# Retention and a gated feed-forward on one core: another order of the ramp, with the powers for q taken from the mask's first row

## Chip, core and metric

The kernel runs on one core of a Trainium2 chip. Its engines are TensorE (PE: matrix products; PEld is its weight load), VectorE (DVE), ScalarE (ACT), GpSimd (POOL) and SyncE (SP, which here only issues DMAs). The metric is the device time of one execution in microseconds (us), as the median of several runs.

## What is computed

Retention in blocks with a decay per head, then RMS norm and a gated feed-forward over its output:

```python
Dmask = np.where(rel >= 0, lam[:, None, None] ** rel[None], 0.0)
lam_pow = lam[:, None, None] ** (pos[None, :, None] + 1)
for b in range(nb):
    intra = np.einsum('bhic,bhjc->bhij', qb, kb) * Dmask[None]
    intra = np.einsum('bhij,bhjd->bhid', intra, vb)
    inter = np.einsum('bhid,bhde->bhie', qb * lam_pow[None], kv_state)
    out[:, :, sl] = intra + inter
    kv_state = lam_block[None, :, None, None] * kv_state + np.einsum(
        'bhsd,bhse->bhde', kb * rev_pow[None], vb)
xn = x / np.sqrt(np.mean(x * x, axis=-1, keepdims=True) + 1e-06) * rms_g
g, val = xn @ w_gate, xn @ w_val
y = (g / (1.0 + np.exp(-g)) * val) @ w_out
```

4 sequences of 768 tokens, 8 heads of 64, a model width of 512 and an inner width of 1536, all float32.

## The kernel before

The 3072 tokens are cut into six groups m of 512, each of four chunks of 128; the heads into four pairs p; the inner width into twelve blocks f of 128. A `Pair(m, p)` does the retention of one group and pair of heads: `scores` (PE, tile pa), `decay_a` (DVE multiplies pa by the mask), `decay_k` (ACT), `decay_q` (POOL, in some places DVE, multiplies q by the powers pw), `state_sums` (PE, pst), `states` (DVE: a copy and multiply-adds), `mix_chunks` and `mix_states` (PE, both into po), `keep_output` and `keep_squares` (po to x and to its squares). `Norm(m)` sums the squares over the heads, takes the root (POOL, a power) and has PE spread it over the partitions (pr); `scaled`, `high` and `low` make the two fp16 parts of x. `Weights(f)` converts the float32 weights of a block, which arrive as pairs of words, into two fp16 parts: `lift` (ACT), `convert` (DVE), `square` (ACT), `norm` (PE, pn), `scale` (DVE), `high` (ACT), `low` (DVE), `undo` (DVE, the factors cg that the silu takes). `Hidden(m, f)` multiplies: `gate` and `val` are twelve fp16 products each, in three parts of four (high by high, low by high, high by low), `silu` and `mul` join them, and `out(t)` multiplies by the block of w_out, one output tile t at a time.

Weights and the first two groups are prepared in a ramp, the function `ramp()`, in which every call stands by itself. It runs under a manual schedule: each engine has one queue and runs its instructions in the order in which `ramp()` issues them, and an instruction that waits holds all behind it on its engine. After the ramp the loop over `unit()` runs the other products; `load_next()` issues the next load on SP's queue.

The places that matter here (lines of the kernel before):

- L155 `powers(p, part)`: parts 0 and 1 are the mask of the pair's two heads, part 2 the powers pw of the pair for q; all twelve are scans on DVE. pw's scans read a tile of zeros that ACT makes (L215).
- L142 `busy(n)`: n products of the identity with itself, which nothing reads.
- L179 to L197 `largest`, `scales`, `scales_of`: the largest norm gain gives the scales gs and cx; `scales_of` is seven small DVE operations.
- L597 `Norm.sums`: for group 0 the squares of pairs 0, 1 and 2 are added first (POOL and DVE, L583), and the two that are left are summed over partitions by products 128 columns wide (`n = 1 if self.m else P`).
- L787 `h1.mul(True)` and L711: h1 isn't split into a high and a low part; its `out` is one float32 product per tile, the others take three products (L714 to L716).

```python
            queue = nc.scalar if m == 0 and p == 0 and i else nc.sync
        n = 1 if self.m else P
```

Of the kernel before, what the change touches and what calls it, by code (L numbers as in the profile page):

```python
# [17 lines left out]
P = 128  # L18
# [5 lines left out]
def retention_swiglu_kernel(  # L24
# [117 lines left out]
    def busy(n):  # L142

        ps = ps_out.tile([P, DM], F32, tag="po2", name="unread")
        for _ in range(n):
            nc.tensor.matmul(ps[:, :P], ident, ident, start=True, stop=True)  # L146
# [8 lines left out]
    def powers(p, part):  # L155
        if part < 2:
            h = 2 * p + part
            nc.vector.tensor_tensor_scan(
                mask[:, h, :], lam_b[:, h : h + 1].broadcast_to([P, P]), ident, 0.0,
                ALU.mult, ALU.add,  # L160
            )
        else:
            nc.vector.tensor_tensor_scan(
                pw[:, p, :], lam_p[:, p : p + 1].broadcast_to([P, P]), zeros, 1.0,
                ALU.mult, ALU.add,
            )
# [23 lines left out]
    def scales_of(pmax):  # L190
        nc.vector.tensor_reduce(gmax, pmax[:, :P], axis=mybir.AxisListType.X, op=ALU.max)
        nc.vector.tensor_single_scalar(ge, gmax.bitcast(I32), 0x7F800000, op=ALU.bitwise_and)
        nc.vector.tensor_scalar_min(ge, ge, float(252 * EXP))
        nc.vector.tensor_scalar(sx.bitcast(I32), ge, -1.0, float(253 * EXP), ALU.mult, ALU.add)
        nc.vector.tensor_scalar(gs, gcol, sx, XS, ALU.mult, ALU.mult)
        nc.vector.tensor_scalar_add(cx.bitcast(I32), ge, float(EXP))
        nc.vector.tensor_scalar_mul(cx, cx, 1.0 / (XS * WS))  # L197
# [15 lines left out]

    zeros = wg[:, NF - 1, 1].bitcast(F32)[:, :P]
    nc.scalar.mul(zeros, ones, 0.0)  # L215
# [141 lines left out]
    class Weights:  # L357
# [79 lines left out]
        def undo(self):  # L437
            inv = small.tile([P, 2], F32, tag="inv", name=f"inv_{self.f}")
            nc.vector.tensor_scalar_add(inv.bitcast(I32), self.e2, float(64 * EXP))
            nc.vector.tensor_scalar_mul(cg[:, self.f, :], inv, cx)  # L440
# [19 lines left out]
    class Pair:  # L460
# [48 lines left out]
        def states(self):  # L509
            m, p = self.m, self.p  # L510
            for c in range(GC):
# [4 lines left out]
                if g % SEQ_CH == 0:  # L516
                    nc.vector.tensor_copy(new, self.pst[:, c, :])
                else:
# [49 lines left out]
        def keep_squares(self):  # L568
# [4 lines left out]
            if m and p == 0:  # L573
# [10 lines left out]

    class Norm:


        def __init__(self, m):
            self.m = m
            self.x, self.sq = rows.pop(m)  # L590
# [6 lines left out]
        def sums(self, i=0):  # L597

            if i == 0:
                if self.m:  # L600
                    pss = ps_att.tile([P, 2, G], F32, tag="ps", name=f"pss_{self.m}")[:, 0]
                else:
                    pss = ps_out.tile([P, DM], F32, tag="po2", name=f"pss_{self.m}")
                self.pss = pss
            sq = self.sq[i]

            n = 1 if self.m else P
            for c in range(GC):
                nc.tensor.matmul(  # L609
                    self.pss[:, c * n : (c + 1) * n], sq[:, c, :], ones[:, :n],  # L610
                    start=i == 0 and c == 0, stop=bool(i or self.m), skip_group_check=True,
                )
            self.pss4 = self.pss[:, : GC * n].rearrange("p (c i) -> p c i", c=GC)[:, :, 0]

        def mean(self):
            m = self.m
            self.ms = small.tile([P, GC], F32, tag="ms", name=f"ms_{m}")
            nc.vector.tensor_scalar(self.ms, self.pss4, 1.0 / DM, 1e-6, ALU.mult, ALU.add)
# [197 lines left out]
    def ramp():  # L816
# [4 lines left out]
        p00, p01, p02, p03, p10, p11, p12, p13 = (Pair(m, p) for m in range(2) for p in range(NP))  # L821
        largest()
        pm = scales()
        powers(0, 0)
        powers(2, 0)
        powers(0, 1)
        powers(1, 1)
        powers(2, 1)
        powers(3, 2)
        powers(3, 1)  # L830
        p00.decay_k()
        busy(5)
        powers(1, 0)
        powers(3, 0)
        powers(0, 2)
        powers(1, 2)
        powers(2, 2)
        p00.scores()
        busy(4)
        p00.decay_a()  # L840
        p00.decay_q(nc.gpsimd)
        p01.decay_k()
        p00.state_sums()
        p00.states()
        p01.scores()
        p01.decay_a()
        scales_of(pm)
        p01.state_sums()
        p01.states()
        p00.mix_chunks()  # L850
        p00.mix_states()
        p02.scores()
        p02.decay_a()
        p02.decay_k()
        p02.state_sums()
        p02.states()
        p01.mix_chunks()
        p01.decay_q(nc.gpsimd)
        p01.mix_states()
        p03.scores()  # L860
        p03.decay_a()
        p00.keep_output(nc.scalar)
        p02.decay_q(nc.gpsimd)
        p00.keep_squares()
        p03.decay_k()
        p03.state_sums()
        p03.states()
        p03.decay_q(nc.gpsimd)
        p01.keep_output(nc.scalar)
        p01.keep_squares()  # L870
        p02.mix_chunks()
        p02.mix_states()
        w0.lift()
        p03.mix_chunks()
        p03.mix_states()
        p02.keep_squares()
        p01.add_squares(nc.gpsimd)
        p02.add_squares(nc.vector)
        w0.convert(part=0)
        w0.convert(part=1)  # L880
        load_next()
        p03.keep_squares()
        p03.keep_output(nc.scalar)
        p02.keep_output(nc.scalar)
        load_next()
        n0 = Norm(0)
        n0.sums(0)
        n0.sums(1)
        w0.square(0)
        n0.mean()  # L890
        w1.lift(0)
        w1.lift(1)
        p10.scores()
        load_next()
        p10.decay_a()
        busy(3)
        busy(8)
        w1.convert(0)
        w0.square(1)
        w0.pn = w1.pn = ps_out.tile([P, DM], F32, tag="po3", name="pn_0")  # L900
        w0.norm()
        w1.convert(1)
        w1.square(0)
        p10.decay_k()
        w0.scale()
        n0.root()
        n0.spread()
        w1.square(1)
        w1.pn = w0.pn[:, 2:]
        w1.norm(slice(0, 1))  # L910
        n0.scaled(0)
        n0.high(0)
        p10.state_sums()
        n0.scaled(1)
        p10.states()
        n0.scaled(2)
        w0.high(0)
        n0.high(1)
        n0.scaled(3)
        w0.low(0)  # L920
        n0.high(2)
        n0.high(3)
        n0.low(1, nc.vector)
        w1.scale(slice(0, 1))
        p10.mix_chunks()
        w0.high(1)
        w0.low(1)
        w0.lift_o()
        w1.high(0)
        n0.low(3, nc.vector)  # L930
        n0.low(2, nc.vector)
        w0.undo()
        w1.low(0)
        w1.pn = ps_att.tile([P, 2, G], F32, tag="ps", name="pn_1")[:, 0]
        w1.norm(slice(1, 2))
        p10.decay_q(nc.gpsimd)
        p10.mix_states()
        h0.gate(0)
        h0.gate(1)
        h0.val(0)  # L940
        w2.lift()
        h0.val(1)
        w1.lift_o()
        n0.low(0, nc.gpsimd)
        h0.gate(2)
        w2.convert(part=0)
        h0.val(2)
        w1.scale(slice(1, 2))
        h0.silu()
        w2.convert(part=1)  # L950
        w1.high(1)
        h0.mul()
        w1.low(1)
# [373 lines left out]
```

## Time and profile before

| | |
|---|---|
| time, median of 3 runs | 678.54 us (677.96 to 679.63) |
| profiled execution, its own time | 678.86 us |
| its span, first to last instruction | 677.1 us |
| mean granted clock of TensorE over the span | 0.999 of full speed |
| busy: PE, DVE, ACT, POOL | 668.6, 328.9, 248.6, 64.1 us |

A busy time is the sum of the times in which an engine has an instruction in work. PE's records overlap (the ends of products are modelled), so the step from one start to the next says what a product costs. A row of the timeline has the start, the time from start to end, engine, line and operation, the tiles (out<-in), sizes and count; in brackets is how long the engine was idle before, and what ended that. Every float32 product is two records in such a row.

### The profile page before, as it was taken

What the parts mean: (1) busy time and instruction counts of PE and PEld (TensorE: products, weight loads), DVE (VectorE), ACT (ScalarE), POOL (GpSimd) and SP (SyncE); (2) the same over time, 40 slices, a digit from 0 to 9 for tenths busy, and PEclk for the clock granted to TensorE, in tenths of its full rate; (3) what the DMA queues carried; (4) which work ended last, traced back from release to release, by engine and by line L of the source; (5) the groups of instructions that cost most, each with busy time, mean ns of one, the idle gap of its engine ahead of it and who ended that gap; (6) DMA issues with size and microseconds to landing.
All of it is one profiled execution on the core that took longest, in us unless ns stands there. A gap on an engine that the chain in (4) does not pass through costs nothing.

```text
span 677.1 us, 9894 instructions
## 1 busy us (share of the span) xinstructions
PE 668.6 (99%) x4138; PEld 362.6 (54%) x4138; DVE 328.9 (49%) x591; ACT 248.6 (37%) x439; POOL 64.1 (9%) x59
## 2 busy tenths in 40 slices
PE   7999999999999999999999999999999999999997
PEld 6845665555566655554444555444465444444443
DVE  6797866466567486453812312641332462211112
ACT  3687635455446324454213222231332231211111
POOL 2300000000012002343000111000012000000000
PEclk9999999999999999999999999999999999999999
DMA  8937802234015101122001132100100000100001
GB/s 312 370 122 277 271 19 99 101 110 153 38 63 178 71 0 63 64 85 104 1 0 46 32 111 67 60 0 1 63 1 1 1 0 1 63 0 1 0 1 62
DMA packets 14301, 50.97 MB, mean 75 GB/s; under 512 B 1713, under 2 KB 1969, under 8 KB 12849
## 3 DMA queue, kind: packets, MB, share of 16 engines
q1 hardware_dynamic: 13968, 49.69, 20.8%
q10 hardware_dynamic: 288, 0.66, 0.3%
q8 instruction: 32, 0.52, 0.3%
q14 instruction: 13, 0.10, 0.0%
HBM read 44.05 MB, written 6.29 MB: 74 GB/s over the span
## 4 chain that ended last, share of the span: by engine, by line
PE 98%; DVE 1%; DMA 0%; ACT 0%; issue 0%; DVEq 0%
PE pg L695 28%; PE pv L695 28%; PE acc L714 10%; PE acc L716 9%; PE acc L715 9%; PE pa L475 4%; PE po L535 3%; PE po L546 3%; PE pst L504 2%; PE unread L146 1%; PE acc L711 1%; DMA cs<-in_consts_dram 0%; PE pss L609 0%; DVE xn L673 0%; PE pr L631 0%; PE pss L645 0%
## 5 line engine op out<-in xcount | busy, mean ns | idle before, releaser
L695 PE MATMUL pg<-x,wg 128*128 128x512 f16 x864 | 199.8, 379 | 0.6 <-ACT x L678 0.6
L695 PE MATMUL pv<-x,wv 128*128 128x512 f16 x864 | 199.5, 379 | 0.0
L787 DVE SCALAR_TENSOR_TENSOR sg<-pv,cv,sg 128x512 f32<-128x512 f32 x48 | 36.0, 750 | 219.6 <-PE pv L695 219.6
L695 PEld LDWEIGHTS <-wv 128*128 128x128 f16 x864 | 84.1, 98 | 100.4 <-issue 1.1
L695 PEld LDWEIGHTS <-wg 128*128 128x128 f16 x864 | 82.3, 98 | 102.9 <-issue 6.1
L716 PE MATMUL acc<-wo,hh 128*128 128x512 f16 (+1 forms) x284 | 109.1, 384 | 0.0
L715 PE MATMUL acc<-wo,hh 128*128 128x512 f16 (+1 forms) x284 | 109.0, 384 | 0.0
L780 ACT ACTIVATE sg<-pg,cg 128x512 f32<-128x512 f32 x72 | 49.4, 685 | 152.3 <-PE pg L695 152.2
L797 ACT CAST hh<-sg 128x512 f16<-128x512 f32 (+1 forms) x71 | 43.9, 618 | 166.1 <-DVE sg L787 166.1
L714 PE MATMUL acc<-wo,hh 128*128 128x512 f16 x192 | 72.9, 380 | 0.0
L495 POOL TENSOR_TENSOR qkv<-qkv,pw 128x512 f32<-128x512 f32 x21 | 27.0, 1285 | 299.3 <-PE pa L475 299.3
L804 DVE TENSOR_TENSOR hh<-sg,hh 128x512 f16<-128x512 f32 x48 | 33.8, 704 | 24.6 <-ACT hh L797 24.6
L714 PE MATMUL acc<-wo,hl 128*128 128x512 f32 x92 | 40.6, 441 | 0.0
L491 DVE TENSOR_TENSOR a<-pa,mask 128x1024 f32<-128x1024 f32 x24 | 29.4, 1224 | 7.6 <-PE pa L475 7.4
L714 PEld LDWEIGHTS <-hh 128*128 128x128 f16 x192 | 18.8, 98 | 23.5 <-issue 2.4
L716 PEld LDWEIGHTS <-hh 128*128 128x128 f16 x192 | 18.8, 98 | 22.7
L787 DVE SCALAR_TENSOR_TENSOR sg<-pv,cg,sg 128x512 f32<-128x512 f32 x23 | 17.2, 748 | 27.3 <-PE pv L695 25.7
L715 PEld LDWEIGHTS <-hh 128*128 128x128 f16 x192 | 18.8, 98 | 20.8
L475 PE MATMUL pa<-qkv 64*128 64x128 f32 x384 | 28.8, 291 | 0.0
L475 PEld LDWEIGHTS pa<-qkv 64*128 64x128 f32 x384 | 24.1, 193 | 8.3 <-issue 7.0
L535 PE MATMUL po<-a,qkv 128*64 128x128 f32 x384 | 25.3, 274 | 0.0
L566 ACT COPY x<-po 128x512 f32<-128x512 f32 x24 | 13.8, 582 | 29.4 <-PE po L546 29.3
(132 smaller groups left out, 615.4 us busy)
## 6 DMA issues: line engine op xcount, KB each, us to landing
qkv<-in_qkv_dram SPq DMA_DIRECT2D x47, 512.0 KB, 5.0
raw_gv<-in_weights_dram SPq DMA_DIRECT2D x11, 1024.0 KB, 6.2
raw_o<-in_weights_dram SPq DMA_DIRECT2D x12, 512.0 KB, 4.0
out_dram<-o SPq DMA_DIRECT2D x23, 256.0 KB, 2.3
partial<-in_weights_dram SPq DMA_DIRECT2D x2, 512.0 KB, 12.5
qkv<-in_qkv_dram ACTq DMA_DIRECT2D x1, 512.0 KB, 4.1
out_dram<-o SPq DMA_DIRECT2D x1, 128.0 KB, 2.1
out_dram<-o ACTq DMA_DIRECT2D x1, 128.0 KB, 2.0
```

The costliest lines, as they stand in the source:

```text
L475: nc.tensor.matmul(self.pa[:, j, c, :], self.kT[r, c, :], self.qT[r, c, :], start=True, stop=True,)
L491: nc.vector.tensor_mul(self.a, self.pa, decay.broadcast_to([P, 2, GC, P]))
L495: eng.tensor_mul(self.qT, self.qT, pw[:, p : p + 1, :].broadcast_to([P, GC, P]))
L535: nc.tensor.matmul(po[r, c, :], self.v[:, c, r], self.a[:, j, c, :], start=c == 0, stop=False, skip_group_check=True,)
L695: nc.tensor.matmul(ps, w[:, kk, :], x[:, kk, :], start=i == kk == 0, stop=i == 2 and kk == NK - 1,)
L714: nc.tensor.matmul(acc, hl[:, ts_], oh, start=first, stop=False)
L715: nc.tensor.matmul(acc, hh[:, ts_], ol, start=False, stop=False)
L716: nc.tensor.matmul(acc, hh[:, ts_], oh, start=False, stop=last)
L780: nc.scalar.activation(self.sg, self.pg, AF.Silu, scale=cg[:, self.f, 0:1])
L787: nc.vector.scalar_tensor_tensor(out, self.pv, factor, self.sg, ALU.mult, ALU.mult)
L797: nc.scalar.copy(self.hh, self.sg)
L804: nc.vector.tensor_sub(self.hl, self.sg, hh)
```

## The change

- **Loads.** Of the first pair's two transfers, qT and kT now go on ACT's queue and k and v on SP's; before it was the other way about.
- **Powers for q.** `spread_powers(p)` has PE multiply the identity's first column, broadcast to 64 columns, by the mask of each of the pair's heads: two products of 64x128, whose result is the mask's first row (powers 0 to 127) on all partitions of a head. `powers_of` lets ACT multiply it by lam into pw. The four DVE scans and the tile of zeros go.
- **Small operations.** `scales_of` (five of seven operations) goes to GpSimd, and so do four of the twelve `undo`s and four `low_o`s (the low part of w_out).
- **Row sums.** `row_sums(m, i)` sums each pair's squares by products one column wide, for group 0 with all four pairs summed on PE: sixteen products in place of eight wide ones, and no `add_squares` for group 0.
- **First weights by halves.** w0 is lifted, converted, squared and scaled half by half (w1 already was).
- **First states.** `first_state` copies a sequence's first state by itself, in five places on ACT.
- **h1** is split like the others (`h1.mul()`, `h1.high()`, `h1.low()`).
- **Fillers** (`busy`): fifteen products in place of twenty, two and five of them ahead of everything else.
- **The order** of all calls in `ramp()` is new.

```diff
-            queue = nc.scalar if m == 0 and p == 0 and i else nc.sync
+            queue = nc.scalar if m == p == i == 0 else nc.sync
...
+    def spread_powers(p):
+        ps = ps_out.tile([P, DM], F32, tag="po3", name=f"pp_{p}")
+        for j, r in enumerate(heads):
+            nc.tensor.matmul(
+                ps[r, :P], ident[:, 0:1].broadcast_to([P, D]), mask[:, 2 * p + j, :], start=True, stop=True
+            )
+        return ps
+
+    def powers_of(p, ps):
+        nc.scalar.mul(pw[:, p, :], ps[:, :P], lam_p[:, p : p + 1])
...
-    zeros = wg[:, NF - 1, 1].bitcast(F32)[:, :P]
-    nc.scalar.mul(zeros, ones, 0.0)
...
+    def row_sums(m, i):
...
+        for c in range(GC):
+            nc.tensor.matmul(
+                pss[m][:, c : c + 1], rows[m][1][i][:, c, :], ones[:, :1],
+                start=i == 0 and c == 0, stop=bool(i == NP - 1 or m), skip_group_check=True,
+            )
...
         largest()
+        powers(3)
+        busy(2, 3)
...
-        h1.mul(True)
...
+        h1.mul()
```

Three places in the order follow: PE at the start, PE from the first group's sums to the first gate, and POOL. Names: unread is a filler, pmax the spread of the largest gain, pa scores, pp the spread powers, pst state sums, po outputs, pss row sums, pn the weights' squared norm, pr the spread root, pg the gate.

PE at its start, before:

```order
L187 MATMUL pmax<-ident,gmax 128x128
L146 MATMUL unread<-ident 128x128 x5
L475 MATMUL pa_0_167<-qkv_0_97 128x128 x8
L146 MATMUL unread<-ident 128x128 x4
L504 MATMUL pst_0_186<-qkv_0_97 64x64 x8
L475 MATMUL pa_1_199<-qkv_1_100 128x128 x8
```

and with the change:

```order
L146 MATMUL unread_146<-ident 128x128 x2
L146 MATMUL unread_150<-ident 128x128 x5
L192 MATMUL pmax<-ident,gmax 128x128
L479 MATMUL pa_0_164<-qkv_0_97 128x128 x8
L146 MATMUL unread_175<-ident 128x128 x2
L165 MATMUL pp_181<-mask,ident 64x128 x2
L508 MATMUL pst_0_185<-qkv_0_97 64x64 x8
```

Seven fillers, which need only the identity, stand ahead of pmax, which needs the constants; the first powers stand behind the first scores.

PE from the last pair's outputs to the first gate (pg), before:

```order
L546 MATMUL po_3_339<-qkv_3_106,state 64x128 x6
L609 MATMUL pss_371<-ones,sq_0_301 128x128 x4
L609 MATMUL pss_371<-ones,sq_3_363 128x128 x4
L475 MATMUL pa_0_389<-qkv_0_360 128x128 x8
L146 MATMUL unread<-ident 128x128 x11
L411 MATMUL pn_421<-ssq_380,ones 128x2
L631 MATMUL pr_436<-ident,y_434 128x128 x4
L411 MATMUL pn_421<-ssq_425,ones 128x1
L504 MATMUL pst_0_447<-qkv_0_360 64x64 x6
L535 MATMUL po_0_473<-a_0_402,qkv_0_360 64x128 x8
L411 MATMUL pn_492<-ssq_425,ones 128x1
L546 MATMUL po_0_473<-qkv_0_360,state 64x128 x6
```

and with the change (the first four products of pg follow):

```order
L558 MATMUL po_3_345<-qkv_3_106,state 64x128 x6
L608 MATMUL pss_297<-ones,sq_1_289 128x1 x4
L608 MATMUL pss_297<-ones,sq_2_379 128x1 x4
L608 MATMUL pss_297<-ones,sq_3_381 128x1 x4
L146 MATMUL unread_402<-ident 128x128 x2
L415 MATMUL pn_405<-ssq_383,ones 128x1 x2
L642 MATMUL pr_426<-ident,y_419 128x128 x4
L479 MATMUL pa_0_433<-qkv_0_280 128x128 x8
L508 MATMUL pst_0_446<-qkv_0_280 64x64 x6
L415 MATMUL pn_405<-ssq_453,ones 128x1
```

The spread root stands ahead of the next group's scores, nine fillers are gone here, and the next group's po comes only after part 0 of the gate.

POOL from the constants on, before:

```order
L495 TENSOR_TENSOR qkv_0_97<-qkv_0_97,pw 128x512
L495 TENSOR_TENSOR qkv_1_100<-qkv_1_100,pw 128x512
L495 TENSOR_TENSOR qkv_2_103<-qkv_2_103,pw 128x512
L495 TENSOR_TENSOR qkv_3_106<-qkv_3_106,pw 128x512
L583 TENSOR_TENSOR sq_0_301<-sq_0_301,sq_1_320 128x512
L622 TENSOR_TENSOR y_434<-ms_383,power 128x4
L495 TENSOR_TENSOR qkv_0_360<-qkv_0_360,pw 128x512
L681 TENSOR_TENSOR x_298<-xn_0_444,x_298 128x512
```

and with the change, from the last two of the five operations of `scales_of` on (which stand between the q of pair 2 and that of pair 3):

```order
L203 TENSOR_SCALAR cx<-ge 128x1
L204 TENSOR_SCALAR cx<-cx 128x1
L499 TENSOR_TENSOR qkv_3_106<-qkv_3_106,pw 128x512
L633 TENSOR_TENSOR y_419<-ms_417,power 128x4
L443 TENSOR_SCALAR inv_458<-e_0_421 128x2
L444 TENSOR_SCALAR cg<-inv_458,cx 128x2
L692 TENSOR_TENSOR x_272<-xn_3_444,x_272 128x512
L692 TENSOR_TENSOR x_272<-xn_2_456,x_272 128x512
L499 TENSOR_TENSOR qkv_0_280<-qkv_0_280,pw 128x512
L443 TENSOR_SCALAR inv_595<-e_1_473 128x2
L444 TENSOR_SCALAR cg<-inv_595,cx 128x2
L257 TENSOR_TENSOR wo_637<-wg,wo_637 128x512
```

Behind the root POOL has two low parts of x in place of one, the factors of w0 and w1, and the low part of the first w_out.

## Rows read from the trace of the kernel before

**Rows 1.** The page's busy times; waits of PE (waited for, total, times, longest).

```profile
PE 668.6 (99%) x4138; PEld 362.6 (54%) x4138; DVE 328.9 (49%) x591; ACT 248.6 (37%) x439; POOL 64.1 (9%) x59
...
PE pmax L187 <- DVE gmax L180: 3.9, 1, 3.9
PE pg L695 <- ACT x L678: 0.6, 2, 0.3
```

**Rows 2.** Timeline, 0 to 10 us: POOL makes the identity, then PE.

```profile
1.12 0.29 POOL masks.py:199 TENSOR_SCALAR_AFFINE_SELECT ident<-ident 128x128 f32<-128x128 f32 x1
...
4.44 2.34 PE L146 MATMUL unread<-ident 128*128 128x128 f32 x10
6.71 2.08 PE L475 MATMUL pa<-qkv 64*128 64x128 f32 x16
8.72 1.54 PE L146 MATMUL unread<-ident 128*128 128x128 f32 x8
```

**Rows 3.** Timeline, PE over one pair, 17.5 to 22 us.

```profile
17.58 1.16 PE L475 MATMUL pa<-qkv 64*128 64x128 f32 x16
...
19.19 1.05 PE L535 MATMUL po<-a,qkv 128*64 128x128 f32 x16
20.16 0.87 PE L546 MATMUL po<-qkv,state 64*64 64x128 f32 x12
20.97 1.09 PE L535 MATMUL po<-a,qkv 128*64 128x128 f32 x16
```

**Rows 4.** Timeline, PE at the first norm, 22 to 30 us.

```profile
22.79 2.05 PE L609 MATMUL pss<-ones,sq 128*128 128x128 f32 x16
...
25.87 3.04 PE L146 MATMUL unread<-ident 128*128 128x128 f32 x22
...
29.06 1.13 PE L631 MATMUL pr<-ident,y 128*128 128x128 f32 x8
```

**Rows 5.** Timeline, the other engines at the first norm, 25 to 32 us.

```profile
25.19 1.03 POOL L622 TENSOR_TENSOR y<-ms,power 128x4 f32<-128x4 f32 x1 [3.83 <-DVE ms L618]
...
30.23 1.40 DVE L673 SCALAR_TENSOR_TENSOR xn<-x,gs,pr 128x512 f32<-128x512 f32 x2 [0.41 <-PE pr L631]
...
31.01 0.62 ACT L678 CAST x<-xn 128x512 f16<-128x512 f32 x1 [0.30 <-DVE xn L673]
...
31.70 1.16 POOL L681 TENSOR_TENSOR x<-xn,x 128x512 f16<-128x512 f32 x1 [4.23 <-ACT x L678]
```

**Rows 6.** Timeline, PE's first products, 32 to 42 us.

```profile
32.73 0.61 PE L695 MATMUL pg<-x,wg 128*128 128x512 f16 x2
...
34.29 1.24 PE L695 MATMUL pg<-x,wg 128*128 128x512 f16 x5 [0.28 <-ACT x L678]
...
38.90 2.75 PE L695 MATMUL pg<-x,wg 128*128 128x512 f16 x12
```

**Rows 7.** Timeline, PE: h1's outputs, narrow row sums of group 1, three-part outputs.

```profile
63.19 1.88 PE L711 MATMUL acc<-wg,h 128*128 128x512 f32 x4
...
81.66 0.95 PE L609 MATMUL pss<-ones,sq 128*128 128x1 f32 x8
82.47 0.48 PE L714 MATMUL acc<-wo,hl 128*128 128x512 f32 x1
...
83.24 0.39 PE L714 MATMUL acc<-wo,hl 128*128 128x512 f32 x1
```

**Rows 8.** Timeline, DVE and POOL, 260.5 to 263 us.

```profile
260.62 0.75 DVE L264 SCALAR_TENSOR_TENSOR rest<-wo,ts,wo 128x512 f32<-128x512 f32 x1
...
261.52 1.27 POOL L267 TENSOR_TENSOR wo<-rest 128x512 f16<-128x512 f32 x1 [28.39 <-DVE rest L264]
...
262.22 1.12 DVE L264 SCALAR_TENSOR_TENSOR rest<-wo,ts,wo 128x512 f32<-128x512 f32 x1 [0.85 <-ACT wo L262]
```

**Rows 9.** DMA issue of w0's two halves on SP's queue.

```profile
5.40 1.24 SPq L98 DMA_DIRECT2D partial<-in_weights_dram  x2
```

**Rows 10.** DMA issues of 5.3 to 5.9 us: KB each, us to landing.

```profile
partial<-in_weights_dram SPq DMA_DIRECT2D x1, 512.0 KB, 12.3
```

More of the change, by code (lines that the diff above doesn't have):

```diff
@@ L889, in ramp @@
-        w0.square(0)
         n0.mean()
-        w1.lift(0)
-        w1.lift(1)
-        p10.scores()
-        load_next()
-        p10.decay_a()
[L896 to L908, printed above, removed]
+        n0.root()
+        w0.scale(slice(0, 1))
@@ new lines, in ramp @@
+        load_next()
+        n0.low(2, nc.gpsimd)
+        w0.high(1)
+        p10.mix_chunks()
+        w1.lift_o()
+        w0.lift_o()
+        p10.first_state(nc.scalar)
+        w1.lift(1)
+        w0.low(0)
+        w0.low(1)
+        n0.low(0, nc.vector)
+        w2.lift()
+        h0.val(0)
+        load_next()
+        n0.low(1, nc.vector)
+        w1.high(0)
+        w2.convert(part=0)
+        h0.gate(1)
+        h0.gate(2)
+        h0.silu()
+        w1.convert(1)
+        w2.convert(part=1)
@@ L933, in ramp @@
+        busy(4)
+        h1.gate(0)
         w1.low(0)
+        p11.decay_k()
+        h0.val(1)
+        w1.square(1)
+        h0.val(2)
         w1.pn = ps_att.tile([P, 2, G], F32, tag="ps", name="pn_1")[:, 0]
         w1.norm(slice(1, 2))
[L936 to L953, printed above, removed]
-        w1.undo()
-        load_next()
-        h1.gate(0)
-        load_next()
-        h1.gate(1)
-        h1.gate(2)
-        h1.val(0)
-        w3.lift()
-        h1.val(1)
         w2.square(0)
         w2.square(1)
+        load_next()
+        w0.convert_o()
+        w1.scale(slice(1, 2))
+        h1.gate(1)
         w2.pn = ps_att.tile([P, 2, G], F32, tag="ps", name="pn_2")[:, 0]
@@ L966, in ramp @@
         w2.norm()
-        h1.silu()
-        w0.convert_o()
-        w2.scale()
+        h1.gate(2)
+        h0.mul()
+        w1.high(1)
+        w2.scale()
+        h1.val(0)
+        w1.low(1)
+        p10.decay_q(nc.gpsimd)
+        w2.high(0)
+        w2.undo(nc.vector)
+        w1.undo(nc.gpsimd)
+        h1.silu()
+        h1.val(1)
+        h2.gate(0)
+        w2.low(0)
+        h2.gate(1)
+        load_next()
+        h2.gate(2)
+        h0.high()
+        w3.lift()
+        p10.states(True)
@@ L1009, in ramp @@
         w3.scale()
[L1010 to L1029 removed]
+        h0.out(0)
@@ L1030, in ramp @@
+        p11.states(True)
+        w3.undo(nc.gpsimd)
+        w3.high(0)
+        h2.val(1)
+        load_next()
+        w4.lift()
+        w2.convert_o()
+        w3.low(0)
+        h3.gate(0)
+        h0.out(3)
+        w4.convert(part=0)
+        p11.decay_q(nc.vector)
+        w3.high(1)
+        h1.high()
+        p12.decay_k()
+        high_o(1)
+        h2.val(2)
+        h2.mul()
         h3.gate(1)
+        w4.convert(part=1)
         h3.gate(2)
-        w4.convert(part=1)
+        h3.silu()
@@ new lines, in ramp @@
+        w3.low(1)
+        h0.out(2)
+        w4.scale()
+        w4.undo(nc.vector)
+        load_next()
+        w4.high(0)
+        p11.keep_output(nc.scalar)
+        h0.out(1)
+        h1.out(0)
+        load_next()
+        p11.keep_squares()
+        p12.states(True)
+        w4.low(0)
+        w3.convert_o()
+        load_next()
+        p12.decay_q(nc.vector)
+        w5.lift()
+        h2.high()
+        h4.gate(0)
+        w4.high(1)
+        h4.gate(1)
+        p13.decay_k()
+        w4.lift_o()
@@ L1052, in ramp @@
[L1052 to L1053 removed]
+        w5.square(0)
+        w5.square(1)
+        p13.scores()
         h3.mul()
[L1055 to L1057 removed]
+        low_o(2, nc.gpsimd)
         p12.mix_chunks()
[L1059 to L1066 removed]
         p12.mix_states()
+        p11.add_squares(nc.gpsimd)
         p12.keep_squares()
[L1069 removed]
```

473 lines of the change are left out of this document (218 added, 255 removed).

## The prediction

> **What bounds the kernel now.** First the busy times: PE is busy for 668.6 of 677.1 us; DVE, next, for 328.9 [rows 1]. Then PE's waits, which are all that PE's idle time can give: 3.9 us before its first product, for the constants, and 0.6 us in two waits at the first gate [rows 1]. So after the ramp a cheaper instruction on another engine buys nothing, and the change can pay in three ways alone: PE starts earlier, PE has less work, or less of that work is padding. What can be lost is a new wait in a stretch that has none now. Last I read the timeline of the first 40 us on all engines, because fillers and half-rate products count as busy: ten passes of fillers take 2.34 us at the start and 22 take 3.04 later, sixteen passes of scores 2.08 and later 1.16 [rows 2 to 4]. The granted clock reads 0.999 over the span, the upper level (2.4 GHz), so the records don't say why; the rows say that PE is slow for some 3.6 us after it starts.
>
> **Start.** The identity is there at 1.41 us [rows 2], so the seven leading fillers begin at 1.5 in place of 3.9. At 0.45 us each (2.34 over five [rows 2]) they end at 4.65; pmax then has its constants, and ends at 5.1. If the slow time is again 3.6 us it is over by then, and pair 0's scores, 1.1 us, end at 6.3; before they ended at 8.72 [rows 2]. **PE is 2.4 us ahead.** If the slow time ends no earlier than now it is 1.5 us less.
>
> **PE's work up to the first norm.** Two fillers 0.5 (a filler is 3.04 over 11, 0.27 [rows 4]). Spread powers: eight products of the shape of an output product, 128 columns on 64, eight of which step 19.19 to 20.16 [rows 3]: 1.0. Three pairs at 3.4 (17.58 to 20.97 [rows 3]) and the rest of pair 0 at 2.4: 12.6. Row sums: four narrow ones step 81.66 to 82.47, 0.8 [rows 7], so sixteen cost 3.2; the eight wide ones cost 2.0 [rows 4]. This part of the change makes PE's work longer, by 1.2; DVE and POOL lose two additions. Sum 17.3, with two short waits that I expect: 0.3 for the first state sums, behind `decay_k`, and 0.2 for pair 3's outputs, whose bank ACT empties only after it has lifted w0's first half, which lands at 17.7 (5.4 plus 12.3, [rows 9, 10]). The sums end at 6.3 + 17.3 + 0.5 = **24.1**; before at 24.8 [rows 4].
>
> **From the norm to the gate.** Here the time is DVE's and ACT's. Mean and root take until 25.4 (a root 1.03 [rows 5] and two hand-overs); pr, a step of 1.0 [rows 4], ends at 26.4, where it used to start at 29.06 behind nine more fillers. DVE must first convert w1's first half and scale w0, so `scaled` begins at 26.8, in the order 3, 2, 0, 1. Each step is 0.66 (two in 1.40 with the tail, [rows 5]); 0 is ready at 28.8 and 1 at 29.5, the casts of 0.62 [rows 5] at 29.5 and 30.15. The gate's part 0 runs from 29.6 to 30.9; before it began at 32.73 and was held until 34.29 [rows 6]. PE meanwhile idles for about two microseconds, since the next pair's outputs, which used to fill this, now follow the gate.
>
> Then po (1.0) and `val` part 0 (0.9, a third of twelve products' 2.75 [rows 6]) to 32.8, and the gate's parts 1 and 2, which want w0's low part and the low parts of x. These are four DVE subtractions of 0.75 at most [rows 8]; without a hold DVE delivers them from 31.9 to 33.8 and the gate ends at 34.5; four fillers, 1.1, lead to 35.6, by when the silu of h0 has let the bank go. h1's gate begins at **35.6**, with parts 1 and 2 of `val` (1.8), the next group's state products (0.8 [rows 3]) and one pn (0.1) still owed, all of which stood before it till now: 38.3 against 38.90 [rows 6], **0.6 ahead**.
>
> **A hold.** When POOL's addition ran at 261.52, a DVE instruction with two inputs from SBUF took 1.12 us, and 0.75 alone [rows 8]: it ended 0.55 after POOL. In the new order POOL has two low parts of x at 1.16 [rows 5] and a q of about 1.27 (as [rows 8]) back to back from 28.6 to 32.1, and DVE's low part of w0, ready at 31.1, is of that kind. If it is held until 32.1, all behind it is a microsecond late: the gate ends at 35.5, h1's gate begins at 36.6, and the balance is 39.3 against 38.90, **0.4 behind**.
>
> The Trainium skill, page "SBUF — State Buffer", section "SBUF: two separate sides", has a rule against this change: DVE and GpSimd share a pair of ports as an exclusive lock, and whichever starts first keeps it for the whole instruction. The trace agrees (1.12 against 0.75). By that rule alone the balance would be the one behind; without it, the one ahead.
>
> I take the middle, 0.1 ahead, because whether the two instructions overlap hangs on some tenths.
>
> **After h1's gate.** h1's outputs become three products for one: four at 0.94 (1.88 for two) against four at 0.77 (82.47 to 83.24) [rows 7]: **0.7 saved** on PE. The cover is DVE's subtraction and ACT's cast for h1, beside PE's work. Fillers: none are left. DVE gives up thirteen small operations and four subtractions to POOL; that costs nothing as long as POOL delivers cg before the silus (by these steps it is 2 us early at the least), and if POOL were late the next gate would stall by as much. A small operation on POOL has no row: it lies between nothing and 1.03, POOL's root of four columns [rows 5]. I take 1.0, its nearest row, and even so the five of `scales_of` and one q behind them end near 20.5, just before pair 3's states; at the lower end 4 us earlier, which gains nothing. ACT gains four powers and five first states; each is shorter than a cast (0.62 [rows 5]), and before the gate they lie in ACT's waits for k and w0. Were that cover gone, up to seven of them, 4 us at that upper bound, would push the gate. The loads: SP's order is the same, the first group's next loads are issued within 3 us of now; w0's first half still ends the load chain at 17.7, covered as above. No other PE wait: there was none after the two at the gate [rows 1], and DVE has less to do.
>
> **Sum.** 0.1 + 0.7 = 0.8 us off the profiled execution's 678.86: 678.06. That execution is 0.32 above the median shown, so 677.7.
>
> **Rivals.**
> 1. *POOL holds DVE through the ramp.* Besides the hold above, four `low_o`s of about 1.25 us each meet DVE's two-input subtractions between 46 and 72 us; by the same stepping PE has 0.3 to 1 us of slack at most gates there. If each costs PE 0.7 and the first hold its full microsecond: 678.54 + 0.4 − 0.7 + 2.8 = 681.0. It decides once DVE's low parts of a block end after PE's part 0 of that gate. For it: the hold in [rows 8]; against: DVE has lost four subtractions and the small operations. Chance 0.13.
> 2. *The waits at the gate vanish.* If ACT and DVE run closer than I step them, the gate starts with the first cast near 28.5, and of the 3 us in which I have PE idle before 35.6 two are saved: 678.54 − 0.6 − 0.7 − 2.0 = 675.2. For it: DVE's two `scaled` take 1.40 [rows 5], less than two steps of 0.75. Against: the chain from root to cast is serial. Chance 0.33, with all between.
> 3. *The change does nothing that PE sees.* The earlier start is eaten by the wider wait (the chain ends at w0's load and the root, not at PE), and only h1's 0.7 stays or goes: 677.8 to 678.5. This is next to the forecast and shares its chance, 0.54 together.
> 4. *PE stays slow at the start until 7.5*, as now by the clock on the wall: 1.5 us less ahead, 679.2 in place of 677.7. Within the middle case.
>
> **How the numbers follow.** A measurement of this kernel can tell about 0.3% (2.0 us) from no change. The likeliest, 677.7, lies within; faster by more needs 676.5, rival 2; slower by more needs 680.6, rival 1. Chances 0.33, 0.54, 0.13. The range reaches from rival 2 (675.0, rounded down) to most of the way to rival 1 (680.2).
>
> **What would show it.** Right: PE's first product at 1.5, the first scores' end near 6.3, row sums' end near 24, the first gate near 29.6 with about 2 us of PE idle ahead of it, h1's gate between 35.6 and 36.6, and no wait of PE beyond. Wrong: DVE subtractions of over 1 us beside POOL and PE waiting for DVE after 40 us (rival 1); a gate before 29 (rival 2); scores of 2 us after 5 us (rival 4).

## The result, and the profile after

The changed kernel takes 680.28 us (median of 12 executions, 678.98 to 681.32), the kernel before 678.92 (12): ratio 1.0016, 95% interval 1.0008 to 1.0023. The forecast was 677.7 us, 0.8 faster; it is 1.4 slower. Over these twelve executions the kernel before stands 0.4 above the median of three that the forecast started from.

First lines of the page of the profiled execution (680.92 us), then PE's waits (waited for, total, times, longest).

```profile
span 677.6 us, 9946 instructions
...
PE 670.6 (99%) x4166; PEld 365.9 (54%) x4166; DVE 322.6 (48%) x569; ACT 250.4 (37%) x447; POOL 74.1 (11%) x77
...
PEclk9899999999999999999999999999999999999999
```

```profile
PE unread L146 <- POOL ident masks.py:199: 1.4, 1, 1.4
PE pst L508 <- ACT sg L791: 0.9, 1, 0.9
PE pg L706 <- ACT x L689: 0.2, 1, 0.2
PE pg L706 <- DVE x L692: 0.2, 1, 0.2
```

PE starts 2.4 us earlier than in [rows 1] and its waits at the gate are shorter, but there is a new one, for a silu, and the clock has a dip in the second slice. PE's timeline:

```profile
1.45 3.36 PE L146 MATMUL unread<-ident 128*128 128x128 f32 x14 [1.45 <-POOL ident masks.py:199]
...
5.16 1.49 PE L479 MATMUL pa<-qkv 64*128 64x128 f32 x16
6.59 0.71 PE L146 MATMUL unread<-ident 128*128 128x128 f32 x4
...
24.06 0.69 PE L146 MATMUL unread<-ident 128*128 128x128 f32 x4
...
26.88 2.08 PE L479 MATMUL pa<-qkv 64*128 64x128 f32 x16
...
30.57 0.81 PE L706 MATMUL pg<-x,wg 128*128 128x512 f16 x3 [0.20 <-ACT x L689]
...
36.26 1.02 PE L706 MATMUL pg<-x,wg 128*128 128x512 f16 x4
...
53.63 1.89 PE L706 MATMUL pg<-x,wg 128*128 128x512 f16 x8
...
57.51 0.57 PE L508 MATMUL pst<-qkv 128*64 128x64 f32 x12 [0.90 <-ACT sg L791]
...
95.68 0.60 PE L706 MATMUL pg<-x,wg 128*128 128x512 f16 x2
```

The first scores end at 6.59, the row sums at 24.06 (the next filler starts), h1's gate begins at 36.26; the row at 53.63 is parts 1 and 2 of h3's gate. The last row is the first unit after the ramp; before, it was this one:

```profile
95.14 1.04 PE L695 MATMUL pg<-x,wg 128*128 128x512 f16 x4
```

So the ramp is 0.54 longer, and the span 0.5; all units after it take the same time. The rest lies outside the span: time less span was 1.73 to 1.86 in every execution of the kernel before, and 2.10 to 3.32 here, median 2.13.

Where PE's new wait comes from, by the chain that ended last (start, us, what):

```profile
45.55 7.73 DMA raw_gv<-in_weights_dram
...
53.30 1.14 ACT w L225
...
56.87 0.59 ACT sg L791
...
57.51 0.57 PE pst L508 x12
```

ACT's lift of w4 waits 2.5 us for its load; h3's silu is queued behind that lift and four other operations, and until it has read h3's gate the state sums of pair 2 can't start. They are put into the gate's bank (a bank is a part of the memory that PE writes): the kernel gives the tag `pg` to every gate and to the state sums of each even pair.

```python
            pool, tag = (ps_out, "po0") if self.odd else (ps_gv, "pg")
...
                self.pg = ps_gv.tile([P, G], F32, tag="pg", name=f"pg_{self.m}_{self.f}")
```

The gate had ended at 55.5. Before, h3's gate ran only after the lift, and its `val` and outputs of h1 stood between it and these state sums:

```profile
57.83 2.94 PE L695 MATMUL pg<-x,wg 128*128 128x512 f16 x12
```

```profile
55.93 1.16 ACT L221 ACTIVATE w<-raw_gv 128x1024 f32<-128x1024 f32 x1 [1.11 <-DMA raw_gv<-in_weights_dram]
```

POOL's hold (a DVE instruction made longer by one on POOL that runs beside it) is there too: DVE's low part of w0 takes 1.53 beside POOL's q. And TensorE's granted clock is at its lower level (1.2 GHz; PEclk, the third column from the end in the rows of windows, counts the upper one as 1) from about 26.4 to 29.8 us, behind the sums of one column.

```profile
31.16 1.53 DVE L437 SCALAR_TENSOR_TENSOR wg<-w,sc,wg 128x512 f16<-128x512 f32 x1
```

```profile
30.86 1.29 POOL L499 TENSOR_TENSOR qkv<-qkv,pw 128x512 f32<-128x512 f32 x1
```

```profile
26.00:28.00 2.00, 2.00 (x17) 1.78 (x17) 1.93 (x6) 1.44 (x5) 0.53 (x2) 0.59 0.99 403
28.00:30.00 2.00, 2.00 (x25) 1.66 (x24) 2.00 (x4) 1.88 (x4) 1.38 (x2) 0.55 1.00 401
```

Theories: **A**, the bank: what is missing is the wait at 57.5. **B**, DVE: it is busy without a gap from 25.5 to 45.5 us, POOL's hold lengthens that, and all later lateness follows. **C**, the clock: its dip (the stretch at the lower level) costs PE's time. Beside them, what lies outside the span.

### The profile page after: what moved, and what is told of

Read it like the earlier page. It is cut to its first block, busy times and chain, and to the rows that moved or that the text cites. A ratio compares the mean times of both kernels' runs of the same rounds, so it can differ in the third digit from the quotient of the medians.

```text
span 677.6 us, 9946 instructions
## 1 busy us (share of the span) xinstructions
PE 670.6 (99%) x4166; PEld 365.9 (54%) x4166; DVE 322.6 (48%) x569; ACT 250.4 (37%) x447; POOL 74.1 (11%) x77
## 4 chain that ended last, share of the span: by engine, by line
PE 94%; DVE 3%; DMA 1%; ACT 1%; issue 0%; POOL 0%; DVEq 0%; SPq 0%; POOLq 0%
PE pv L706 26%; PE pg L706 26%; PE acc L725 10%; PE acc L727 9%; PE acc L726 9%; PE pa L479 3%; PE po L547 3%; PE po L558 3%; PE pst L508 2%; DMA raw_gv<-in_weights_dram 1%; PE unread L146 1%; PE pss L608 1%; DVE w L237 0%; DVE wg L437 0%; DVE xn L684 0%; DVE w L234 0%
## 5 line engine op out<-in xcount | busy, mean ns | idle before, releaser
L727 PE MATMUL acc<-wo,hh 128*128 128x512 f16 (+1 forms) x288 | 110.7, 384 | 0.0
L726 PE MATMUL acc<-wo,hh 128*128 128x512 f16 (+1 forms) x288 | 110.6, 384 | 0.0
L725 PE MATMUL acc<-wo,hl 128*128 128x512 f32 x96 | 42.5, 442 | 0.0
L547 PE MATMUL po<-a,qkv 128*64 128x128 f32 x384 | 25.5, 275 | 0.0
L489 ACT ACTIVATE qkv<-qkv,mask 128x256 f32<-128x256 f32 x48 | 21.6, 499 | 4.7 <-DVE mask L156 3.5
```

The costliest lines, as they stand in the source:

```text
L547: nc.tensor.matmul(po[r, c, :], self.v[:, c, r], self.a[:, j, c, :], start=c == 0, stop=False, skip_group_check=True,)
L725: nc.tensor.matmul(acc, hl[:, ts_], oh, start=first, stop=False)
L726: nc.tensor.matmul(acc, hh[:, ts_], ol, start=False, stop=False)
L727: nc.tensor.matmul(acc, hh[:, ts_], oh, start=False, stop=last)
```

## The experiments

Below, each ratio is to the kernel before, "outside" is the median of time less span, and "low" counts executions whose mean granted clock is 0.997 or less; there was none among the executions of the kernel before.

**The kernel before, again.** 

> The kernel before, unchanged, to learn the span of several of its executions. The changed kernel's span was 677.6 us in the profiled execution and 676.8 to 679.2 over twelve; the time of an execution lay 2.1 to 3.3 us above its span. For the kernel before one pair is known, 678.86 and 677.1, so 1.76. If the loss lies within the span, the spans here are near 677.1 and time and span differ by 2.1 or more here too. If part of it lies outside the span, the difference here stays at 1.7 to 1.8.

679.05 us, ratio 1.0003 (0.9994 to 1.0011); median span 677.25, outside 1.79, low 0 of 12. Part of the loss is outside the span.

**The bank** (ramp of the changed kernel):

```diff
-        p12.state_sums()
         p11.mix_chunks()
         p11.mix_states()
         w3.lift_o()
+        p12.state_sums()
```

> The changed kernel, with the state sums of the next group's pair 2 behind pair 1's output products in place of ahead of them. Theory A (the missing microsecond is PE's wait at 57.5 us: the state sums take the bank of h3's gate, and its silu has not read it yet): 1.9 us of PE's work stands in front, the wait of 0.96 goes to nothing, the unit after the ramp starts near 94.7 in place of 95.68, and the time falls by 0.9. Theory B (the delay is on DVE and in the loads, and shows wherever PE next needs them): the wait turns up again within 10 us, at the first outputs or at h4's gate, and the time falls by under 0.3.

679.39 us, ratio 1.0013 (1.0003 to 1.0023); median span 677.15, outside 2.23, low 12 of 12. PE's list of waits:

```profile
PE unread L146 <- POOL ident masks.py:199: 1.4, 1, 1.4
PE pg L706 <- ACT x L689: 0.7, 2, 0.4
PE pg L706 <- DVE x L692: 0.2, 1, 0.2
```

```profile
36.70 1.02 PE L706 MATMUL pg<-x,wg 128*128 128x512 f16 x4
...
95.30 2.76 PE L706 MATMUL pg<-x,wg 128*128 128x512 f16 x12
```

The wait is gone and does not come back: from h1's gate to the unit after the ramp 58.60 us in place of 59.42. That is A, with 0.82 for 0.96. (0.96: the scores ahead of the state sums start at 55.45 and usually step on after 1.1, and the state sums start at 57.51.) The span of this execution gains half of it: here the dip of the clock fell on pr, which all of the norm waits for, and h1's gate began 0.44 later:

```profile
25.37 2.08 PE L642 MATMUL pr<-ident,y 128*128 128x128 f32 x8
```

**POOL's q to DVE:**

```diff
-        p10.decay_q(nc.gpsimd)
...
         h0.low()
+        p10.decay_q(nc.vector)
```

> The changed kernel, with the q of the next group's pair 0 scaled by DVE behind h0's low part (about 45 us) in place of by POOL at 30.9 us, where DVE's low part of w0 took 1.45 us beside it. Theory B (DVE is busy without a gap from 25.5 to 45.5 us, POOL's hold of 0.8 is in this chain, and it ends in the load of w4): w0's low part takes 0.75, h1's gate starts at 35.5 in place of 36.26, w4's load is issued at 44.8 in place of 45.55, PE's wait at 57.5 shrinks by most of it, and the time falls by 0.7 to 1.4. Theory A alone: h1's gate is earlier, and the wait at 57.5 longer by as much, so the time stays within 0.3.

679.22 us, ratio 1.0013 (0.9998 to 1.0028); median span 677.35, outside 1.90, low 10 of 12.

```profile
31.51 0.74 DVE L437 SCALAR_TENSOR_TENSOR wg<-w,sc,wg 128x512 f16<-128x512 f32 x1
```

```profile
PE pst L508 <- ACT sg L791: 0.7, 1, 0.7
```

```profile
30.91 0.81 PE L706 MATMUL pg<-x,wg 128*128 128x512 f16 x3 [0.28 <-ACT x L689]
...
36.27 1.02 PE L706 MATMUL pg<-x,wg 128*128 128x512 f16 x4
```

The hold is gone (0.74 for 1.53), but from the gate's second product to h1's gate that gives only 0.33 (5.36 us for 5.69): PE no longer waits for DVE there, and the rest of the hold had cost it nothing. w4's load is issued 9.29 us behind h1's gate, as in the changed kernel (45.56 less 36.27, 45.55 less 36.26). DVE follows PE there, and the wait at 57.5 is only 0.2 shorter, so B's second half falls.

**Wide sums** (`n = P` for group 0 in `row_sums`):

```diff
-                pss[m][:, c : c + 1], rows[m][1][i][:, c, :], ones[:, :1],
+                pss[m][:, c, :], rows[m][1][i][:, c, :], ones[:, :n],
```

> The changed kernel, with the first group's row sums 128 columns wide, as in the kernel before, in place of one column; all sixteen products stay. Theory C (the lower granted clock from 26 to 30 us, behind products of one column, costs PE's time): the clock stays at the upper level, the scores at 26.9 take 1.2 us in place of 2.08, and the time falls by 1 to 1.5. Theories A and B: PE waits for DVE there anyway, the first gate stays at 30.0, and the time is the same within 0.3, or up to 0.5 longer by the wider products.

679.46 us, ratio 1.0009 (0.9999 to 1.0019); median span 677.2, outside 2.14, low 1 of 11.

```profile
26.00:28.00 2.00, 2.00 (x31) 1.76 (x31) 1.93 (x6) 1.43 (x4) 0.54 (x2) 1.00 0.99 389
28.00:30.00 2.00, 0.84 (x15) 0.57 (x10) 2.00 (x4) 1.88 (x4) 1.51 (x2) 1.00 0.97 391
```

The dip is gone, and PE's idle time ahead of the gate, which the slow products had filled, comes to light (1.4 us in its list of waits). h1's gate starts 0.14 earlier: in the changed kernel's traced execution the dip was hidden, as A and B said. It costs time in executions where it lasts longer (below).

**The small operations back on DVE** (`scales_of`, `undo`, `low_o` with `nc.vector` for `nc.gpsimd`).

> The changed kernel, with the five operations of the scales, four undo and four low parts of the output weights back on DVE, as in the kernel before. The first group's scales and one undo lie in DVE's idle time; three undo of 0.4 and four subtractions of 0.7 come back into DVE between 40 and 90 us. The prediction's step (these cost nothing on POOL): the span stays within 0.5 of the changed kernel's 677.6. Rival 1 (POOL holds DVE at each low part of the output weights): the span falls by 1 or more. For the time outside the span (1.8 in the kernel before, 2.1 in the changed kernel, and in its trace two fetches of instructions after the last output): if it hangs on the length of POOL's program, which here is again that of the kernel before, it returns to 1.8; if on PE's or ScalarE's, it stays at 2.1.

682.95 us, ratio 1.0058 (1.0046 to 1.007); median span 681.1, outside 1.77, low 5 of 5. Neither of the two cases expected this.

```profile
29.13 1.13 DVE L444 TENSOR_SCALAR cg<-inv,cx 128x2 f32<-128x2 f32 x1
```

```profile
29.09 2.27 POOL L692 TENSOR_TENSOR x<-xn,x 128x512 f16<-128x512 f32 x2 [3.71 <-ACT x L689]
```

```profile
26.00:28.00 2.00, 2.00 (x12) 1.78 (x12) 1.59 (x5) 1.44 (x3) 0.00 (x0) 0.50 1.01 414
...
32.00:34.00 2.00, 1.93 (x8) 0.61 (x8) 1.97 (x5) 2.00 (x6) 0.59 (x1) 0.50 0.00 0
```

A multiplication of two columns on DVE takes 1.13 us beside POOL, 0.9 more than its other executions (0.23), on the path to the last two parts of x, and the clock stays low from 25 to 35 us, so that the gate itself runs slowly. Not every small operation is held: in the changed kernel one of a single column, which reads one tile, took its usual 0.15 beside POOL's q (at 31.09). What separates the two wasn't tested.

**No leading fillers:**

```diff
-        busy(2, 3)
         powers(0)
-        busy(5)
```

> The changed kernel, without the seven leading fillers (14 passes) that PE does while it waits for the constants. The prediction's step (PE is slow for some 3.6 us after it starts, so an early start makes pair 0's scores end at 6.3): PE starts near 3.9 and is slow until 7.5, the first scores end near 7.6 in place of 6.6, the row sums end near 25 in place of 24.06, and the span grows by up to 1.0. Rival (PE's early lead is lost in waits for ScalarE, DVE and w0's load before the first norm): the row sums end by 24.5 and the span is the same within 0.3. Outside the span: PE's program is 28 instructions shorter; if the second fetch after the last output is PE's, it is gone and no execution has 3 us outside.

681.78 us, ratio 1.0042 (1.0029 to 1.0055); median span 679.6, outside 2.17, low 5 of 5. The sums end at 26.4 in place of 24.06, 0.7 of it because the constants landed later in this execution. The other 1.6 is more than expected, because PE stays slow for longer: pair 1's scores, 5.5 us after PE's start, still take 1.56 for the 1.09 of later ones.

```profile
10.09 1.63 PE L479 MATMUL pa<-qkv 64*128 64x128 f32 x16
11.65 1.09 PE L547 MATMUL po<-a,qkv 128*64 128x128 f32 x16
```

In the median the span is 2.0 longer, so the early start is passed on. How much of the 2.0 is its worth alone is open: three of the five executions have a clock of 0.994, which none of the changed kernel's has. The second fetch after the end is gone and no execution has 3 us outside. That says nothing of whose fetch it was: the trace of the bank's run, with as many instructions on PE as the changed kernel (4166), lacks it too, and none of its twelve executions has 3 us.

**The three edits together** (bank, q, wide sums).

> The changed kernel with the three edits together: wide row sums, the next group's first q on DVE, pair 2's state sums behind pair 1's output products. Theories A, B and C each claim a part, in the span: 0.96 for the wait at 57.5 us, 0.45 for POOL's hold at 31 us as measured at h1's gate, and up to 0.5 in executions whose clock is low behind the row sums. If they add up, h1's gate starts near 35.7, PE has no wait after 36 us, the unit after the ramp starts near 94.1 in place of 95.68, the span is 676.1 to 676.4 and the time 678.0 to 678.4, 0.6 below the kernel before. If what one edit gives comes back as another wait, the span stays near 677.1.

678.41 us, ratio 0.9997 (0.9986 to 1.0007); median span 676.6, outside 1.81, low 2 of 12.

```profile
PE unread L146 <- POOL ident masks.py:199: 1.5, 1, 1.5
PE pg L708 <- ACT x L691: 1.4, 2, 1.2
PE pr L644 <- POOL y L635: 0.2, 1, 0.2
```

```profile
30.52 0.81 PE L708 MATMUL pg<-x,wg 128*128 128x512 f16 x3 [0.28 <-ACT x L691]
...
35.88 1.02 PE L708 MATMUL pg<-x,wg 128*128 128x512 f16 x4
...
94.49 2.76 PE L708 MATMUL pg<-x,wg 128*128 128x512 f16 x12
```

They add up: the end of the ramp is 1.19 earlier, 0.81 of it behind h1's gate (A) and 0.33 between the gate's second product and h1's gate (5.36 us again: the hold).

**The kernel before with three products for h1** (`h1.mul()`, `h1.high()`, `high_o(1)`, `h1.low()`, `low_o(1, nc.vector)`, the last four between 47 and 51 us).

> The kernel before, with one part of the change alone: h1's outputs as three products in place of one. The prediction's term: 0.7 less of PE's work, the span 677.1 to 676.4, the time 678.2. By the changed kernel's timeline the outputs take 0.71 each in place of 0.94, so 0.9. Against: two subtractions more on DVE (1.4 us) and two casts on ScalarE between 47 and 53 us; if a gate then waits for them, nothing is left. Outside the span: 1.8 as before.

678.18 us, ratio 0.9989 (0.998 to 0.9997); median span 676.4, outside 1.79, low 0 of 11. The term stands, 0.8 of span, and no gate waits.

**Outside the span: POOL's program.** Two constants by ScalarE (`nc.scalar.mul(power, ones[:, :GC], -0.5)`, `nc.scalar.copy(one, ones[:, :1])`).

> The changed kernel, with two constants of 128x4 and 128x1 set by ScalarE in its idle start in place of by POOL, so that POOL's program has two instructions less (77 to 75) and DVE's and PE's stay as they are. Outside the span the kernels showed 1.8 us with POOL at 59 to 64 instructions, 1.8 to 1.9 at 76 and 2.1 to 2.2 at 77. If that time hangs on POOL's program, it is 1.8 here, and the span stays at 677.6 or within 0.4 of it. If on DVE's (which differed in the same kernels), it stays at 2.1.

680.06 us, ratio 1.002 (1.0009 to 1.0031); median span 677.75, outside 2.14, low 11 of 12. A shorter program on POOL alone does not bring 1.8 back.

**The small operations on DVE, with wide sums.**

> The run with the small operations back on DVE (span 681.1, clock 0.992, low from 25 to 35 us), and the first group's row sums 128 columns wide besides. Theory C (the low clock behind one-column row sums made 2.5 of its 3.5 us; the rest is DVE's undo of w0, held for 0.9 by POOL's low part of x): the clock reads 0.999, w0's undo still takes 1.1, h1's gate starts near 37.0, the span is 678.2 to 678.6. If the hold alone made the loss: the span stays at 680 or more.

681.94 us, ratio 1.004 (1.0025 to 1.0055); median span 680.05, outside 1.89, low 5 of 6. The profiled execution, the one at full clock, does what C said: span 678.6, h1's gate at 37.25. At full clock the move back to DVE thus costs 1.4 (678.6 for the 677.2 of wide sums alone), 0.8 of it between the sums' end and h1's gate (12.93 for 12.11), where the hold is. The other five are low all the same, with spans of 679.1 to 681.0, and the median falls by only 1.05 of the 2.5 that C claimed. So products of one column aren't the only thing that the lower clock follows. In the traced execution PE's wait ahead of the gate is the longest of all:

```profile
31.28 0.38 PE L708 MATMUL pg<-x,wg 128*128 128x512 f16 x1 [2.32 <-ACT x L691]
```

**Part 1 of val for the fillers ahead of h1's gate** (on the three edits).

```diff
-        busy(4)
+        h0.val(1)
         h1.gate(0)
...
-        h0.val(1)
```

> The run with the three edits (span 676.6), with part 1 of h0's val where the four fillers ahead of h1's gate stand, and the fillers left out. PE's work before h1's gate stays the same but for 1.0 of fillers: h1's gate starts near 35.8 as before, with 0.87 less owed behind it, the span falls to 675.7 and the time to 677.5, which would be 1.5 below the kernel before. Against: the pn of w1's second half moves ahead by as much, and DVE and ScalarE, which follow PE from there, may then be the late ones at h1's gate parts or h0's outputs; then under 0.4 is left.

678.14 us, ratio 0.9987 (0.9979 to 0.9996); median span 676.3, outside 1.79, low 1 of 11. It gives 0.3 to 0.6 (69.82 from the end of the sums to the end of the ramp, for 70.39), less than its 0.87; what took the rest wasn't followed.

**The early start in the old order** (kernel before with three products; `busy(7)` ahead of `largest()`, `busy(5)` gone, the four fillers behind the first scores kept; the loads swapped).

> The kernel before with h1's outputs as three products (span 676.4), and the start of the changed kernel besides: seven leading fillers while PE waits for the constants, none behind them, and the first q and k on ScalarE's queue. The changed kernel lost 2.0 us of span when its leading fillers went. If PE's early start is worth as much in the old order: scores end at 6.4 in place of 8.7, the span is 674.5. If the chain there ends at w0's load, the squares and the root (rival 3 of the prediction): the eleven fillers at the first norm and its waits take it up, and the span stays within 0.4 of 676.4.

677.77 us, ratio 0.9979 (0.997 to 0.9988); median span 675.95, outside 1.82, low 1 of 12. Between both, nearer to the second. PE has two new waits in the profiled execution:

```profile
PE pa L475 <- DVE a L491: 1.5, 1, 1.5
...
PE pg L695 <- ACT wg L429: 1.3, 1, 1.3
```

**The same, with these two places mended** (against the run just shown):

```diff
-        powers(0, 2)
-        powers(1, 2)
-        powers(2, 2)
         p00.scores()
         busy(4)
         p00.decay_a()
+        powers(0, 2)
...
         p00.states()
+        powers(1, 2)
...
         scales_of(pm)
+        powers(2, 2)
...
         w3.high(1)
-        w4.lift()
         p11.mix_chunks()
         w3.high(0)
         w3.lift_o()
+        w4.lift()
```

> The kernel before with three products for h1 and the early start (677.8, spans 674.4 to 677.3), and two places in its order mended where PE waited in that run's trace: pair 0's decayed scores ahead of the powers for q on DVE (PE waited 1.5 us at 10.1), and the lift of w4 behind w3's high part on ScalarE (PE waited 1.35 at 58.4 for that high part, which stood behind a lift whose weights landed late). If these two waits ate the early start, both are gone, the row sums end near 22.7 and the span is 674.0 to 675.0. If the chain through w0's load, the squares and the root is the end anyway, only the second is worth something, in the executions that had it: the span stays near 675.5 and its spread shrinks.

676.99 us (676.83 to 677.24), ratio 0.997 (0.996 to 0.998): only 0.3%, but each of the seven executions is faster than every one of both kernels. Median span 675.2, outside 1.79, low 0 of 7. Both waits are gone, the second in exchange for 0.6; the sums end at 22.73. Against the run with three products alone the early start gives 1.2 of span, half of the 2.4 that PE starts earlier.

```profile
PE pg L695 <- DVE wg L433: 0.6, 1, 0.6
```

**Outside the span: DVE's program** (`nc.vector.memset(one, 1.0)` for POOL's).

> The changed kernel, with one constant of 128x1 set by DVE in its idle start in place of by POOL: DVE has 570 instructions in place of 569, nothing else moves. Outside the span all kernels with 569 on DVE showed 2.13 to 2.2 (POOL at 77 or 75), all with 570 or more 1.8 to 1.9. If that time hangs on DVE's program, it is 1.8 to 1.9 here, with the span as in the changed kernel, 677.6. If it is something else that the moved q brought, it stays at 2.1.

679.09 us, ratio 1.0006 (0.9995 to 1.0016); median span 677.3, outside 1.82, low 11 of 12. The time outside goes with DVE's program: the medians are 2.13 to 2.23 in all five kernels with 569 instructions there, 1.77 to 1.90 in all with 570 or more, where single executions still reach 2.1. Nine executions have spans of 676.7 to 677.9, at a clock of 0.997 or above; the three at 0.995 have 678.9 to 679.5. The traced one is of these: its clock is low from 24.0 to 30.9 us, from within the row sums on, and h1's gate begins at 38.58 in place of 36.26. So a longer dip can cost 2 us; it doesn't always, as the run with q on DVE has spans of 676.7 to 677.7 at clocks of 0.994 to 0.996 too.

**Narrow sums in the kernel before.**

```diff
-            n = 1 if self.m else P
+            n = 1
```

> The kernel before, with the first group's eight row sums of one column in place of 128, as the change has them; its fillers and its order stay. If products of one column alone bring the low clock (theory C in its narrow form), the clock reads 0.995 to 0.997 and pr, the scores and the first gate take longer. If it takes PE's waits behind them too (in the new order PE waits 0.3 to 2.3 us between the sums and the first gate, here 22 fillers stand there), the clock stays at 0.999 to 1.0 and the span within 0.3 of 677.1.

679.86 us, ratio 1.0008 (0.9998 to 1.0018); median span 678.1, outside 1.79, low 7 of 12. So one-column sums bring the dip without waits behind them, in some executions; the median span grows by 0.9, and the seven low ones, at 678.0 to 678.7, lie above the other five, at 676.3 to 677.9. The fillers after them take half as long again as in [rows 4]:

```profile
25.40 4.57 PE L146 MATMUL unread<-ident 128*128 128x128 f32 x22
```

```profile
26.00:28.00 2.00, 1.94 (x9) 1.65 (x9) 1.97 (x4) 1.25 (x4) 1.00 (x1) 0.50 1.01 416
```

## Why the prediction was wrong

The step that failed is that PE would meet no other wait behind h1's gate. Term by term:

- **Start: right in its result, partly by luck.** Scores ended at 6.59 for 6.3. But that PE is slow for 3.6 us is not what the rows say: in [rows 2] the scores that end at 8.72, 4.8 us after PE's start, all take 2.01 for the 1.09 of later ones. In the changed kernel pair 0's were still slow in part (1.43), and without the leading fillers pair 1's too (1.56). The lead is worth 1.6 us at the sums' end (by the run without the leading fillers); in the old order 1.2 reach the end of the program, in the new one that isn't parted from the clock.
- **PE's work up to the norm: right**, sums' end 24.06 for 24.1.
- **Norm to gate: right in its times** (29.99 for 29.6; h1's gate 36.26, between the two cases), wrong in its picture: PE spent most of the two idle microseconds on products at half clock.
- **Hold: there in full, smaller in its price**: 0.8 on DVE, but 0.33 at h1's gate for the 1.0 put down, as the rest had slack on PE. The Trainium skill, page "SBUF — State Buffer", section "SBUF: two separate sides", has a rule for it: of a GpSimd operation and a DVE one that is in a 2-port mode, or that has two SBUF inputs while GpSimd's reads SBUF, whichever starts first keeps the shared ports for its whole instruction. The trace agrees for the low part of w0, which has two such inputs: 1.53 beside POOL's q, 0.74 without it. The 1.13 for two columns fits as well; by which of the two conditions no run here shows. Rival 1's other holds, at the low parts of the output weights, made no wait of PE: the time is near rival 1's 681.0, by other causes.
- **h1's outputs: right**, 0.7 forecast, 0.8 of span measured.
- **Small operations: right that they cost nothing on POOL, wrong that nothing hangs on them.** Left on DVE in this order they cost 3.5 us of span in the median, 1.4 at full clock.
- **"No other PE wait": the step that failed.** It was argued from the waits of the old order and from DVE's load. The new order brings h3's gate forward to where ACT still waits for w4's load, and puts the next state sums, which use that gate's bank, only one set of scores behind it, so that they wait for its silu: 0.96, of which 0.82 came back when they were moved.
- **Not in the sum at all:** the clock's dip behind one-column sums, which the prediction priced as PE's work alone (1.2 us more), and 0.35 outside the span.

The profiled span then reads: 36.26 plus the 2.7 owed is 0.06 behind [rows 6], less 0.7, plus 0.96: 0.3 later; measured 0.54, and 0.2 is not itemised. With 0.35 outside that is 0.9 for a usual execution; the median's 1.4 has besides it three executions with 3 us outside and those with a lower clock. Where the 3 us come from stays open. The one trace of such an execution has two fetches of instructions behind its last output; the bank's run has one of them, and 2.15 us outside. The two rows are from the DMA queues' view of its end (queue and kind, packets, MB, share):

```profile
q8 instruction: 1, 0.02, 0.4%
q14 instruction: 1, 0.01, 0.2%
```

## What to carry to other kernels

A list of waits says nothing on an order in which a consumer stands earlier: for each product that is moved, ask which bank it writes, who must read that bank first, and which load stands ahead of that reader in its queue. Let PE do its fillers while it waits at its start (1.2 us of span in the old order, with the two new waits mended), and look at the granted clock of every stretch whose products you make narrower. A tiny DVE operation beside a long POOL one can cost what is left of POOL's: here 1.13 us for 0.23.

## What the runs showed of the hardware that was not expected

- Products of one column, which leave PE busy in the records, are mostly followed by a stretch at the lower clock: in the new order 62 of 70 executions with one-column sums are low, and 9 of 40 with wide ones (5 of these with the small operations on DVE, where the traced execution, at full clock, waited 2.3 us ahead of the gate); in the old order 7 of 12 with one-column sums, none of the kernel before, and 1 of the 30 with wide sums and other edits. The stretch differs in length: 26.4 to 29.8 us in the changed kernel's trace, 25 to 35 with the small operations on DVE.
- One instruction moved from POOL to DVE, in idle time, made the median time outside the span 0.3 us shorter (2.13 to 1.82). Why wasn't settled.
- PE is slow after its start for a time that differs from run to run: in the changed kernel into pair 0's scores, 4 us after the start, and without leading fillers into pair 1's, 5.5 us after it.
